# An mLSTM and MLP kernel: the output stores of steps 2 to 6 go from ScalarE's DMA queue to SyncE's

## The chip, the cores and the metric

The kernel runs on one core of a Trainium2 chip. The metric is device time in microseconds for one execution, lower being better. A core has a matrix engine (TensorE, PE), three engines for elementwise work (VectorE or DVE, ScalarE or ACT, GpSimd or POOL) and SyncE (SP), which here does nothing but issue DMAs. Each engine runs its own stream of instructions in order. A DMA is issued by an instruction in the stream of one of them (ACT's and SP's here); the transfer itself runs on 16 DMA engines, which both streams share.

## The reference

The input holds 4 batches of 8 heads with 768 time steps and head size 40. For each head an mLSTM recurrence runs over the time steps, with gates in the log domain and a running maximum for stability. Its output, 3072 rows (batch and time) of 320 values, goes through an MLP of width 2048:

```python
for t in range(S):
    m_new = np.maximum(f_gate[:, :, t] + m, i_gate[:, :, t])
    f_stab = np.exp(f_gate[:, :, t] + m - m_new)
    i_stab = np.exp(i_gate[:, :, t] - m_new)
    C = f_stab * C + i_stab * outer(v[t], k[t])      # per batch and head
    n = f_stab * n + i_stab * k[t]
    y[t] = sigmoid(o_gate[t]) * (C @ q[t]) / max(abs(n @ q[t]), 1)
...
h = x @ w_in          # x: y as (3072, 320), w_in (320, 2048)
g = h * sigmoid(h)
out = g @ w_out       # w_out (2048, 320)
```

All inputs and the output are float32.

## The kernel before

**Units and steps.** The recurrence is done in chunks of 64 time steps (`L`). There are 12 chunks and two pairs of batches, so 24 units; a unit holds one chunk of two batches and all heads, 128 rows of the MLP's input. Three units (`UPS`) make a step: 384 rows that go through the MLP together. There are 8 steps (`NSTEP`), numbered 0 to 7 by `j`.

**The MLP in a step.** The width 2048 is cut into 16 groups of 128, counted by `fc`. For each group `mm1` (L743) makes `ph`, 128 x 384, in a PSUM bank; `act` makes the gated value from it: the tanh on ACT (L750), `(th + 1) * ph` on DVE (L764), and from step 1 on a split into a rounded high part `gh` (ACT, L769) and the low rest `gl` (DVE, L773). `mm2` (L794) then multiplies with `w_out` and accumulates over all 16 groups into three PSUM banks `pout`, one for each 128 rows. It runs two groups behind `mm1` (`LAG`), so the last two groups of step `j` are multiplied while `fc` is 0 and 1 in step `j + 1`. In steps 1 to 7 three matmuls stand for one product, to keep float32 accuracy.

**The store.** When the last group of a step has been accumulated, which is at `fc = 1` of the next step, `store` copies each `pout` bank to SBUF as `ob` (ACT, L814; the very last copy of all is on DVE, L812) and issues two DMAs of 64 rows each (L818), one for each batch of the pair. So a step has three copies and six stores. `ob` has three buffers, except in the last step, which takes larger ones from another pool. The three `pout` banks are written again by `mm2` of the new step at `fc = 2`, and each must have been copied by then. Before the change, the stores of steps 0 and 1 are issued by SP, those of steps 2 to 6 by ACT, and in step 7 one of each two by SP and the other by ACT.

**The units in between.** The attention units of step `j + 1` are worked on inside step `j`: in steps 1 to 6 at `fc` 2, 7 and 12 (`PLACES`). There `block` puts the unit's matmuls on TensorE (scores L511, values L583 and L598, state L648), `close` and the calls after it do the weighting (L538), the norm (L611 to L621) and `x` (L635) on DVE, and `carry` updates the state (POOL L668, DVE L674). One group later `turn` transposes `x` on TensorE (L690), and ACT and DVE put it down as the high and low input of the next step (L701, L702). The first of these three places comes right behind the stores of the step before.

**What sets the order.** The order on each engine is the order in which the code is written; all engines are scheduled by hand. On SP, `turn(n)` issues the loads for unit `n + 3`: two DMAs for `D` (L430), one for `qk` (L438), one for `ko` (L445), two for `vb` (L451), and then two for `lq` of unit `n + 2` (L464). Buffers are few: `D`, `ko` and `vb` rotate over three, `lq` over two, so a load waits until a unit before it has been read. The weights are loaded and prepared in step 0 and partly step 1. After the last units (21 to 23) are reached, `turn` has fewer loads to issue, and step 7 has none.

What each engine does around a step boundary, in written order: TensorE has `mm1(0)`, `mm2(14)` of the old step, `mm1(1)`, `mm2(15)` of the old step, `mm1(2)`, the unit's matmuls, `mm2(0)`, `mm1(3)`, `mm2(1)`, the transposes. ACT has the three copies with whatever DMA issues stand behind each, then the tanh of `fc = 2`, `gh`, and so on.

Of the kernel before, what the change touches and what calls it, by code (L numbers as in the profile page):

```python
# [29 lines left out]
NSTEP = NU // UPS  # L30
# [13 lines left out]
def mlstm_mlp_kernel(  # L44
# [11 lines left out]
    nc = tc.nc  # L56
# [649 lines left out]
    class Step:  # L706
# [97 lines left out]
        def store(self, t):  # L804
            n = self.j * UPS + t
            c, p = n // NP, n % NP
            if self.j < NSTEP - 1:
                ob = p3.tile([128, DM], F32, tag="ob", name=f"ob{n}")
            else:
                ob = pb.tile([128, DM], F32, tag="big", name=f"ob{n}")  # L810
            if self.j == NSTEP - 1 and t == UPS - 1:
                nc.vector.tensor_scalar(ob, self.po[t], 0.5, None, op0=ALU.mult)  # L812
            else:
                nc.scalar.activation(ob, self.po[t], AF.Copy, scale=0.5)  # L814
            for k in range(2):
                r = (2 * p + k) * S + c * L
                q = nc.sync if self.j in (0, 1) or self.j == NSTEP - 1 and k == 0 else nc.scalar
                q.dma_start(out[r : r + L, :], ob[k * L : (k + 1) * L])  # L818


# [281 lines left out]
```

## Time and profile before

| | |
|---|---|
| median of 3 executions | 464.67 us (464.63 to 466.96) |
| the profiled execution | 465.99 us |
| its span, first to last instruction | 464.1 us |
| mean granted TensorE clock | 0.989 of full speed |
| busy share of PE, DVE, ACT, POOL | 96%, 58%, 46%, 25% |

How such rows are read. In a row of the timeline the first number is the start in microseconds from the span's start, the second the duration, then the engine, the line of the code, the operation and its tiles, a count where several were merged, and in brackets how long the engine had been idle before and what ended that. ACTq and SPq are the sequencers of ACT and SP, so a row with ACTq and DMA_DIRECT2D is a DMA being issued, not its transfer. In a row of the waits stand the waiting engine and line, what it waited for, the total in microseconds, how often, and the longest. In a row of windows stand the window, its length, then busy time and number of instructions for PE, PEld (weight loads), DVE, ACT and POOL, and at the end the granted TensorE clock, the mean busy share of the DMA engines and GB/s. A row of a line gives the shortest, median and longest duration in nanoseconds and the first and the last start. The chain of work is followed back from the last instruction to what released it.

### The profile page before, as it was taken

Reading aid. Unit: us, or ns where it says so; the run is one execution under the profiler, and the core shown is the slowest. Engines: PE = TensorE matmul, PEld = TensorE weight load, DVE = VectorE, ACT = ScalarE, POOL = GpSimd, SP = SyncE. Lnnn points to the kernel's source line nnn. Section 1 sums busy time; section 2 is a strip of 40 time slices with the busy share of each in tenths; the row PEclk is TensorE's granted clock in tenths of the full one; section 3 lists DMA queues with packets and bytes.
Section 4 is the critical chain, followed back from the end, with each engine's and each line's share of the span. In section 5 each row is a group of like instructions: output and inputs, shape, how many; then the busy total and the mean of one; then the engine's idle time right before and its main releaser. Section 6 shows DMA issues by size and latency. Waiting matters only on the chain.

```text
span 464.1 us, 11033 instructions
## 1 busy us (share of the span) xinstructions
PE 445.1 (96%) x4477; PEld 408.8 (88%) x4477; DVE 269.8 (58%) x609; ACT 212.1 (46%) x442; POOL 115.6 (25%) x123
## 2 busy tenths in 40 slices
PE   7899999999999999979999899998999899999995
PEld 3667677899999999979999799998999799998995
DVE  5777799578775566444664555636655355533342
ACT  6674856444753442525424344434344344333332
POOL 4224234134142234131431332322332311000000
PEclk9899999999999999998999999999999999998999
DMA  8999896361331442141430522413313200001001
GB/s 211 320 295 274 235 265 148 97 159 49 81 122 40 127 122 65 59 110 56 124 101 22 148 63 76 123 48 118 122 31 93 62 1 2 2 12 32 0 1 42
DMA packets 27314, 47.03 MB, mean 101 GB/s; under 512 B 4160, under 2 KB 14464, under 8 KB 27264
## 3 DMA queue, kind: packets, MB, share of 16 engines
q1 hardware_dynamic: 24224, 43.45, 33.6%
q10 hardware_dynamic: 3040, 2.89, 2.3%
q8 instruction: 35, 0.57, 0.5%
q14 instruction: 15, 0.12, 0.1%
HBM read 42.30 MB, written 4.01 MB: 100 GB/s over the span
## 4 chain that ended last, share of the span: by engine, by line
PE 83%; DMA 6%; DVE 3%; ACTq 3%; ACT 2%; issue 1%; SPq 0%; DVEq 0%
PE ph L743 37%; PE pout L794 35%; DMA wro<-in_w_out_dram 3%; ACTq L818 3%; PE p L598 3%; DMA qk<-in_qk_dram 3%; PE p L511 2%; PE pu L648 2%; PE p L583 2%; PE p L690 2%; ACT ob L814 1%; ACT th L750 1%; DVE th L764 1%; DVE D L538 1%; PE pt L193 0%
## 5 line engine op out<-in xcount | busy, mean ns | idle before, releaser
L750 ACT ACTIVATE th<-ph 128x384 f32<-128x384 f32 x128 | 62.4, 487 | 139.8 <-PE ph L743 132.7
L764 DVE SCALAR_TENSOR_TENSOR th<-th,ph 128x384 f32<-128x384 f32 x112 | 62.1, 555 | 107.5 <-ACT th L750 106.9
L743 PE MATMUL ph<-xh,wh 128*128 128x384 f32 x336 | 116.3, 346 | 0.0
L743 PE MATMUL ph<-xl,wh 128*128 128x384 f32 x336 | 114.6, 341 | 0.0
L794 PE MATMUL pout<-woh,gh 128*128 128x320 f32 x336 | 106.5, 317 | 2.2 <-ACT ob L814 2.2
L794 PE MATMUL pout<-woh,gl 128*128 128x320 f32 x336 | 104.2, 310 | 0.0
L794 PE MATMUL pout<-wol,gh 128*128 128x320 f32 x336 | 103.7, 308 | 0.0
L773 DVE TENSOR_TENSOR gl<-th,gh 128x384 fp32r<-128x384 f32 x112 | 64.6, 577 | 47.5 <-ACT gh L769 47.5
L769 ACT CAST gh<-th 128x384 fp32r<-128x384 f32 x112 | 57.5, 513 | 74.9 <-DVE th L764 74.3
L743 PE MATMUL ph<-xh,wl 128*128 128x384 f32 x224 | 76.6, 342 | 0.0
L794 PEld LDWEIGHTS pout<-woh,gh 128*128 128x128 f32 x336 | 63.6, 189 | 5.5 <-ACT ob L814 3.4
L495 POOL TENSOR_TENSOR qt<-qk,lq 104x512 f32<-104x512 f32 x22 | 29.5, 1340 | 141.5 <-ACT lq L491 125.0
L743 PEld LDWEIGHTS ph<-xl,wh 128*128 128x128 f32 x336 | 63.8, 190 | 0.2
L743 PEld LDWEIGHTS ph<-xh,wh 128*128 128x128 f32 x336 | 63.7, 190 | 0.2
L794 PEld LDWEIGHTS pout<-wol,gh 128*128 128x128 f32 x336 | 63.5, 189 | 0.0
L794 PEld LDWEIGHTS pout<-woh,gl 128*128 128x128 f32 x336 | 63.5, 189 | 0.0
L668 POOL TENSOR_TENSOR Cm<-Cm,lq 40x328 f32<-40x328 f32 x40 | 30.2, 756 | 114.5 <-PE p L598 113.0
L743 PEld LDWEIGHTS ph<-xh,wl 128*128 128x128 f32 x224 | 42.6, 190 | 0.0
L794 PE MATMUL pout<-wo,g 128*128 128x320 f32 x96 | 28.8, 436 | 0.6 <-DVE wo L261 0.6
L482 POOL TENSOR_TENSOR D<-D,am 128x512 f32<-128x512 f32 x20 | 25.8, 1288 | 7.4 <-DMA D<-LFd 5.4
L474 POOL TENSOR_TENSOR am<-mask,aT 128x512 f32<-128x512 f32 x20 | 23.2, 1160 | 7.8 <-DVE aT L203 6.3
L743 PE MATMUL ph<-x,wi 128*128 128x384 f32 x64 | 23.8, 494 | 0.0
(113 smaller groups left out, 485.6 us busy)
## 6 DMA issues: line engine op xcount, KB each, us to landing
qk<-in_qk_dram SPq DMA_DIRECT2D x24, 416.0 KB
ko<-in_ko_dram SPq DMA_DIRECT2D x24, 320.0 KB
wro<-in_w_out_dram SPq DMA_DIRECT2D x8, 640.0 KB
D<-LFd SPq DMA_DIRECT2D x40, 128.0 KB
wri<-in_w_in_dram SPq DMA_DIRECT2D x8, 512.0 KB
vb<-in_vp_dram SPq DMA_DIRECT2D x48, 82.0 KB
out_dram<-ob ACTq DMA_DIRECT2D x33, 80.0 KB
lq<-LFd SPq DMA_DIRECT2D x20, 128.0 KB
```

Of the source, the lines that this page charges most:

```text
L474: nc.gpsimd.tensor_tensor(out=self.am, in0=mask.unsqueeze(1).broadcast_to([128, H, L]), in1=aT[:, self.c, self.p, :].unsqueeze(2).broadcas ...
L482: nc.gpsimd.tensor_tensor(out=self.Dm, in0=self.Dm, in1=self.am, op=ALU.add)
L495: nc.gpsimd.tensor_tensor(out=self.qt, in0=self.q, in1=self.lq, op=ALU.mult)
L598: nc.tensor.matmul(self.out[g * L : (g + 1) * L, d, :, e, :], self.qt[:, j, :], cm[:, :, j, :], start=False, stop=True, skip_group_check=True,
L668: nc.gpsimd.tensor_tensor(out=v, in0=v, in1=self.lq[r, :, L - 1].unsqueeze(2).broadcast_to([D, H, D1]), op=ALU.mult,)
L743: nc.tensor.matmul(ph, w, x, start=(i == 0), stop=(i == len(ops) - 1))
L750: nc.scalar.activation(th, ph, AF.Tanh, scale=0.5)
L764: nc.vector.scalar_tensor_tensor(out=th, in0=th, scalar=1.0, in1=ph, op0=ALU.add, op1=ALU.mult)
L769: nc.scalar.copy(gh, th)
L773: nc.vector.tensor_tensor(out=gl, in0=th, in1=gh.bitcast(F32), op=ALU.subtract)
L794: nc.tensor.matmul(self.po[t], g[:, ts], w, start=(fc == 0 and i == 0), stop=(last and i == len(ops) - 1),)
L818: q.dma_start(out[r : r + L, :], ob[k * L : (k + 1) * L])
```

## The change

The condition that picks the issuing engine of a store is shortened. Every store of steps 0 to 6 is now issued by SP; in step 7 it stays as it was. The copies, the tiles, the sizes and all other instructions are the same, and the order in which the code writes them down is the same on all engines.

```diff
@@ -814,7 +814,7 @@
                 nc.scalar.activation(ob, self.po[t], AF.Copy, scale=0.5)
             for k in range(2):
                 r = (2 * p + k) * S + c * L
-                q = nc.sync if self.j in (0, 1) or self.j == NSTEP - 1 and k == 0 else nc.scalar
+                q = nc.sync if self.j < NSTEP - 1 or k == 0 else nc.scalar
                 q.dma_start(out[r : r + L, :], ob[k * L : (k + 1) * L])
```

## The prediction

> **What bounds the kernel now.** I read the page first: the busy shares and the chain of work that ended last.
>
> ```profile
> span 464.1 us, 11033 instructions
> PE 445.1 (96%) x4477; PEld 408.8 (88%) x4477; DVE 269.8 (58%) x609; ACT 212.1 (46%) x442; POOL 115.6 (25%) x123
> ...
> PE ph L743 37%; PE pout L794 35%; DMA wro<-in_w_out_dram 3%; ACTq L818 3%; PE p L598 3%; DMA qk<-in_qk_dram 3%; PE p L511 2%; PE pu L648 2%; PE p L583 2%; PE p L690 2%; ACT ob L814 1%; ACT th L750 1%; DVE th L764 1%; DVE D L538 1%; PE pt L193 0%
> ```
>
> TensorE sets the time; what can be won is the part of the span in which it idles or is clocked down. But L818, the line that issues the stores, stands on the chain with 3% as ACTq: ScalarE's sequencer issuing DMAs. So the next views are where those issues are made, and who makes TensorE wait between 190 and 430 us:
>
> ```profile
> L818 ACTq DMA_DIRECT2D out_dram<-ob x33: 472/549/1674, 197.4 to 460.6; - x33
> L818 SPq DMA_DIRECT2D out_dram<-ob x15: 502/587/1656, 92.7 to 460.6; - x15
> ```
> ```profile
> PE p L690 <- DVE x L635: 7.1, 4, 2.4
> PE pout L794 <- ACT ob L814: 2.2, 4, 1.0
> ```
>
> One issue holds its queue for a median 549 ns on ACT, 587 ns on SP. From 190 us on TensorE waits twice four times, 9.3 us together; the same question over 90 to 196 us has no row at all. Eight steps of 128x3 rows each end in six stores, and the stores of steps 0 and 1 are on SP already. So the trace holds the changed order too: the step boundaries at 92 and 145 us have their stores on SP, those at 197, 254, 308, 362 and 415 us on ACT. The timeline of one of each kind, SP's first:
>
> ```profile
> 144.76 1.08 ACT L814 ACTIVATE ob<-pout 128x320 f32<-128x320 f32 x3
> 145.22 4.82 SPq L818 DMA_DIRECT2D out_dram<-ob  x6
> 145.96 0.49 ACT L750 ACTIVATE th<-ph 128x384 f32<-128x384 f32 x1
> 150.12 1.19 SPq L430 DMA_DIRECT2D D<-LFd  x2
> 150.16 0.68 DVE L635 SCALAR_TENSOR_TENSOR x<-ko,p 128x256 f32<-128x256 f32 x3
> 152.30 0.49 PE L690 MATMUL p<-ident,x 128*128 128x128 f32 x3
> ```
> ```profile
> 196.99 0.43 ACT L814 ACTIVATE ob<-pout 128x320 f32<-128x320 f32 x1
> 197.45 1.19 ACTq L818 DMA_DIRECT2D out_dram<-ob  x2
> 198.76 0.44 ACT L814 ACTIVATE ob<-pout 128x320 f32<-128x320 f32 x1 [1.34 <-PE ph L743]
> 200.94 0.44 ACT L814 ACTIVATE ob<-pout 128x320 f32<-128x320 f32 x1 [1.74 <-PE pu L648]
> 203.35 0.49 ACT L750 ACTIVATE th<-ph 128x384 f32<-128x384 f32 x1 [1.97 <-DMA out_dram<-ob]
> 207.28 0.55 PE L690 MATMUL p<-ident,x 128*128 128x128 f32 x3 [2.44 <-DVE x L635]
> ```
>
> With the stores on SP, ACT copies all three output tiles in 1.08 us and starts the next tanh (L750) 1.20 us after the first copy. With the stores on ACT, two issues stand behind each copy and the tanh starts 6.36 us after it. The releasers printed there (ph, pu) had long been done; the time between the copies is the issues. VectorE runs in written order: its L764 needs that tanh, the norm of the attention unit stands behind it, x comes last, and TensorE's transposes (L690) wait 2.44 us.
>
> **The change part by part.** Thirty issues (steps 2 to 6, six each) go from ACT to SP. No instruction, tile or byte is added. The gain per boundary is read by windows from the first output copy to the transposes, all with the same 128 to 130 matmuls (the last has no unit, below):
>
> ```profile
> 92.21:100.04 7.83, 7.83 (x130) 7.42 (x130) 5.86 (x16) 3.09 (x8) 4.02 (x4) 1.00 0.41 102
> 144.76:152.30 7.54, 7.54 (x129) 7.12 (x128) 5.51 (x14) 2.57 (x7) 4.01 (x4) 1.00 0.34 88
> 196.99:207.28 10.29, 7.85 (x129) 7.00 (x128) 3.83 (x12) 2.70 (x7) 3.81 (x4) 1.00 0.41 118
> 253.59:263.40 9.81, 7.97 (x129) 7.02 (x127) 3.83 (x12) 2.70 (x7) 3.81 (x4) 1.00 0.42 122
> 308.15:317.08 8.93, 7.70 (x129) 7.02 (x127) 3.83 (x12) 2.70 (x7) 3.82 (x4) 1.00 0.46 134
> 361.86:371.93 10.07, 7.96 (x129) 7.03 (x128) 3.83 (x12) 2.69 (x7) 3.80 (x4) 1.00 0.27 72
> ```
>
> The first number is the window's length, the second TensorE's busy time in it. In the two SP boundaries these are equal: nothing is left to win there. I take 7.54 as the price of a changed boundary, because the one at 92 us holds two split instructions of the first weights besides; 7.83 is the upper bound. The four excesses are 2.75 + 2.27 + 1.39 + 2.53 = 8.94 us (7.78 by the upper bound).
>
> What follows each stall, from the transposes to the next first copy:
>
> ```profile
> 152.30:196.99 44.69, 44.69 (x444) 43.85 (x442) 24.94 (x55) 19.54 (x42) 11.94 (x11) 1.00 0.33 92
> 207.28:253.59 46.31, 46.31 (x442) 45.47 (x443) 26.28 (x57) 19.63 (x42) 11.94 (x11) 0.96 0.26 77
> 263.40:308.15 44.75, 44.75 (x442) 43.91 (x443) 26.19 (x57) 19.42 (x42) 11.94 (x11) 1.00 0.29 80
> 317.08:361.86 44.78, 44.77 (x442) 43.94 (x443) 25.80 (x56) 19.41 (x42) 11.94 (x11) 1.00 0.27 80
> ...
> 209.00:211.00 2.00, 2.00 (x8) 2.00 (x8) 1.22 (x3) 1.16 (x3) 0.00 (x0) 0.50 0.74 259
> ```
>
> After the 2.44 us stall the granted clock (last but two) falls to 0.50, and the stretch takes 46.31 instead of 44.69: 1.62 us. The others lose 0.06 and 0.09, which I leave out. Without a stall no row shows such a drop, so I count 1.62.
>
> The last boundary (step 6 to 7) has no unit in it; its matmuls are read singly:
>
> ```profile
> 413.36 0.31 PE L794 MATMUL pout<-woh,gh 128*128 128x320 f32 x1
> 414.68 0.34 PE L743 MATMUL ph<-xh,wh 128*128 128x384 f32 x1
> 416.09 0.31 PE L794 MATMUL pout<-woh,gh 128*128 128x320 f32 x1
> 419.06 0.42 PE L794 MATMUL pout<-woh,gh 128*128 128x320 f32 x1 [1.00 <-ACT ob L814]
> 419.63 0.52 PE L743 MATMUL ph<-xh,wh 128*128 128x384 f32 x1
> 423.87 0.34 PE L743 MATMUL ph<-xh,wh 128*128 128x384 f32 x1
> ```
>
> Nine pout matmuls take 414.68 - 413.36 = 1.32 us, eight ph ones 416.09 - 414.68 = 1.41. From 416.09 to 423.87 lie pout, ph, pout: 4.05 us of work in 7.78, so 3.73 lost, partly to waiting for the copies (a PSUM bank is written again only once it is copied), partly to the halved clock (0.52 us against 0.34 for one matmul). With three copies in 1.08 us from 415.15 on, all banks are free at 416.23, before the second is due; I count the whole 3.73. Its lower bound is the waits alone, 2.2.
>
> A rule of the Trainium skill bears on the clock: TensorE: Matmul & The Clock Gate (Part 1: The HAM clock gate) has the clock halve after an idle window of about 3.4 us, free-running. The trace agrees on the half (0.50) but drops after 2.44 us of idling. By that rule neither gap would need to cost anything, and the drop terms (1.62, and about 1.5 of the 3.73) would be luck of the phase; the sum would be near 11.2 us and the time 454.8, inside the range.
>
> **What the move costs on SP.** The six issues hold SP 4.82 us there (3.7 to 4.8 in the two boundaries), and behind them in SP's order stand the loads of the next turn: D, qk, ko, the two halves of vb, lq. They cannot pass a store that waits for its copy.
>
> ```profile
> SPq L430 <- PE p L583: 125.7, 13, 11.4
> SPq L445 <- DVE x L635: 33.9, 13, 6.2
> ```
> ```profile
> 167.20 1.29 POOL L482 TENSOR_TENSOR D<-D,am 128x512 f32<-128x512 f32 x1
> ```
>
> Both first loads wait in any case, D's for the unit's matmuls (L583) and ko's for x. In the SP boundary the D load is issued at 150.12 to 151.31, some 3 us later in the boundary than it could be, and its first reader is POOL at 167.20: 15.9 us of cover. lq, issued last, is wanted two mm1 groups after the next unit and has about as much (estimate from the spacing of 2.73 us). So I cost the move at nothing; the bounds are 0 and, if the cover were gone, the 4.82 us per boundary. After step 5 only the lq load of the last unit remains, after step 6 none.
>
> **Sum:** 8.94 + 1.62 + 3.73 = 14.29 us, between 7.78 + 2.2 = 10.0 and 14.3. The profiled execution took 465.99 (span 464.1 and 1.9 around it): 465.99 - 14.29 = 451.7. The median is 464.67, 1.3 below it: 450.4 if that is an offset of the profiled run, 451.7 if it is one clock drop more, which the change would remove too. I take the middle, **451.0**.
>
> **The rivals.**
>
> 1. *A remainder stays* (chance 0.08). x then comes late from VectorE's own chain. In the SP boundary x is done at 150.84 and TensorE wants it at 152.30: 1.46 us of slack. Were x later than that by 1 us in four boundaries, with one clock drop and the lower 2.2 in the last, 14.29 - 4 - 1.62 - 1.53 = 7.14 remain, 7.15 less than counted: 451.0 + 7.15 = 458.2. For it: ACT and DVE alternate tightly. Against: two boundaries without any wait.
>
> 2. *The transfer is hidden anyway* (0.03). ACT is busy 46%, so the issues could lie in its idle time and the waits have another cause: 464.7. Against it stand the 1.97 us which the tanh waits for the stores, and the undisturbed SP boundaries. This is what the Trainium skill would lead one to: DMA: Bandwidth & Descriptors (Issuing engines are not separate DMA queues) says that the choice of issuer saves only the sequencer's time, usually small beside the DMA. Six issues in an engine's in-order stream are what this trace shows to be not small.
>
> 3. *Slower* (0.03): SP becomes the bound. Loads behind the stores arrive after their reader, POOL's L482, then the exponential, the weighting and the block on TensorE slip. The point is a delay of 15.9 us; past it each microsecond is paid at the four boundaries that load, so 19.5 us late (4 x 3.6 = 14.4) ends even and, 5 us past the point, 451.7 + 20 = 472. SP's queue shows 4.82 us of stores, a third of the cover.
>
> 4. *The stores stay tied to ACT* (0.01), by a wait that the written order keeps: as before, 464.7.
>
> **How the numbers follow.** The forecast has 0.85. Its own range is 449 to 454 (the median's 450.4 less a little, up to 10.0 us of gain less 451.7's offset: 465.99 - 10.0 = 456.0 at the most). The full range 449 to 456.5 takes those bounds in and leaves about 0.15 out: the rivals. About 0.5%, 2.3 us, is what a measurement can tell from no change. Faster 0.93 (forecast and rival 1), same 0.04 (2 and 4), slower 0.03 (3).
>
> **What would show it.** On ACT, three copies back to back and the tanh 1.2 us after the first at all seven boundaries; no row of PE waiting for x or ob after 190 us; windows of 7.5 us at the four boundaries and a granted clock of 1.00 after them; 45 stores on SPq, three on ACTq. L818 leaves the chain but for the tail. Wrong would be a POOL or ACT wait on D, lq or qk after a boundary, an x still late, or a clock drop without a stall.

## The result, and the profile after

The changed kernel takes 451.72 us (median of 4, 451.30 to 453.48) against 464.93 for the kernel before (median of 4, 464.63 to 466.96). The ratio is 0.9714, 95% interval 0.9676 to 0.9752: some 2.9% faster. The forecast was 451.0 in a range of 449.0 to 456.5. The profiled execution took 451.44 us, and the sum in the prediction, made against the profiled execution before, gave 451.7 for it.

The page of the changed kernel, busy shares and the chain by line:

```profile
span 449.6 us, 11053 instructions
...
PE 439.1 (98%) x4477; PEld 405.3 (90%) x4477; DVE 270.9 (60%) x609; ACT 211.5 (47%) x442; POOL 116.2 (26%) x123
...
PE ph L743 40%; PE pout L794 39%; PE p L598 3%; DMA wro<-in_w_out_dram 3%; DMA qk<-in_qk_dram 3%; PE p L511 3%; PE pu L648 2%; PE p L583 2%; PE p L690 2%; PE pt L193 0%; ACT ob L814 0%; DVE wo L261 0%; ACT wro L260 0%; ACTq L818 0%; SPq L107 0%
```

L818 on ACTq has gone from 3% of the chain to none, and the waits of TensorE between 80 and 450 us have no row left. The stores now stand on SP's queue, but for three in step 7:

```profile
L818 SPq DMA_DIRECT2D out_dram<-ob x45: 466/587/1665, 92.7 to 446.2; - x45
L818 ACTq DMA_DIRECT2D out_dram<-ob x3: 497/550/792, 444.5 to 446.2; - x3
```

The boundary behind step 2, in the timeline:

```profile
197.00 1.08 ACT L814 ACTIVATE ob<-pout 128x320 f32<-128x320 f32 x3
198.19 0.49 ACT L750 ACTIVATE th<-ph 128x384 f32<-128x384 f32 x1
...
197.45 3.99 SPq L818 DMA_DIRECT2D out_dram<-ob  x6
201.54 2.07 SPq L430 DMA_DIRECT2D D<-LFd  x2
...
204.54 0.49 PE L690 MATMUL p<-ident,x 128*128 128x128 f32 x3
```

The three copies stand back to back, the tanh starts 1.19 us after the first (6.36 before), and the transposes come without a wait. The windows from the first copy to the transposes at the four changed boundaries with a unit (columns as before: window, length, busy time by engine, granted clock, DMA share, GB/s):

```profile
197.00:204.54 7.54, 7.54 (x130) 7.12 (x129) 5.52 (x14) 2.57 (x7) 4.01 (x4) 1.00 0.33 86
249.25:256.80 7.55, 7.55 (x130) 7.13 (x129) 5.52 (x14) 2.58 (x7) 4.02 (x4) 1.00 0.36 98
301.48:309.02 7.54, 7.54 (x129) 7.12 (x128) 5.51 (x14) 2.57 (x7) 4.02 (x4) 1.00 0.36 92
353.74:361.28 7.54, 7.54 (x129) 7.12 (x128) 5.51 (x14) 2.58 (x7) 4.02 (x4) 1.00 0.33 87
```

They equal the 7.54 us of the undisturbed boundary of before, so 10.29 + 9.81 + 8.93 + 10.07 us has become 30.17: 8.93 us. The stretch behind the first of them and the last step, from its first copy to that of the next:

```profile
204.54:249.25 44.71, 44.71 (x444) 43.87 (x442) 24.94 (x55) 19.53 (x41) 11.94 (x11) 1.00 0.34 92
404.42:444.07 39.65, 39.65 (x251) 39.65 (x250) 16.14 (x29) 15.16 (x32) 0.00 (x0) 1.00 0.05 13
```

The first was 46.31 before (1.60 less), the second 43.37:

```profile
415.15:458.52 43.37, 41.70 (x251) 41.18 (x250) 16.14 (x29) 15.38 (x32) 0.00 (x0) 0.96 0.05 12
```

That is 3.72 less. 8.93 + 1.60 + 3.72 = 14.25 of the 14.5 us between the two spans.

**What varies, and what doesn't.** The first output copy of all comes between 92.1 and 95.8 us in the executions of this study, though nothing differs between the kernels up to there. From that copy on the same code takes the same time within some 0.03 us: step 1, for example, is 52.22 or 52.23 us whenever its two boundaries are undisturbed. So the experiments below are read by windows that start at a copy, and the medians, which also hold the spread of the beginning, stand beside them. Each experiment ran in a round with the kernel before, whose median was between 463.86 and 466.39 us in these rounds, so medians of different rounds are comparable to some tenths of a per cent only.

### The profile page after: what moved, and what is told of

Read it like the earlier page. It is cut to its first block, busy times and chain, and to the rows that moved or that the text cites. A ratio compares the mean times of both kernels' runs of the same rounds, so it can differ in the third digit from the quotient of the medians.

```text
span 449.6 us, 11053 instructions
## 1 busy us (share of the span) xinstructions
PE 439.1 (98%) x4477; PEld 405.3 (90%) x4477; DVE 270.9 (60%) x609; ACT 211.5 (47%) x442; POOL 116.2 (26%) x123
## 4 chain that ended last, share of the span: by engine, by line
PE 92%; DMA 6%; ACT 0%; issue 0%; DVE 0%; ACTq 0%; SPq 0%
PE ph L743 40%; PE pout L794 39%; PE p L598 3%; DMA wro<-in_w_out_dram 3%; DMA qk<-in_qk_dram 3%; PE p L511 3%; PE pu L648 2%; PE p L583 2%; PE p L690 2%; PE pt L193 0%; ACT ob L814 0%; DVE wo L261 0%; ACT wro L260 0%; ACTq L818 0%; SPq L107 0%
## 5 line engine op out<-in xcount | busy, mean ns | idle before, releaser
L794 PE MATMUL pout<-woh,gh 128*128 128x320 f32 x336 | 105.4, 314 | 0.0
L773 DVE TENSOR_TENSOR gl<-th,gh 128x384 fp32r<-128x384 f32 x112 | 65.6, 586 | 47.5 <-ACT gh L769 47.5
L794 PEld LDWEIGHTS pout<-wo,g 128*128 128x128 f32 x96 | 17.7, 189 | 7.3 <-DVE wo L261 1.9
```

The source lines that it names most:

```text
L773: nc.vector.tensor_tensor(out=gl, in0=th, in1=gh.bitcast(F32), op=ALU.subtract)
L794: nc.tensor.matmul(self.po[t], g[:, ts], w, start=(fc == 0 and i == 0), stop=(last and i == len(ops) - 1),)
```

## The experiments

**One boundary put back, behind step 2.**

```diff
-                q = nc.sync if self.j < NSTEP - 1 or k == 0 else nc.scalar
+                q = nc.sync if self.j != 2 and (self.j < NSTEP - 1 or k == 0) else nc.scalar
```

> The changed kernel, but the six stores of step 2 go out on ACT again, so one boundary (near 197 us) is as it was before. Theory (the issues in ACT's in-order stream delay the tanh, and with it x): that boundary takes 10.3 us again instead of 7.5, and where the clock drops after it 1.6 more; 451.7 + 2.75 = 454.5, or 456.1 with the drop. Rival (what was won does not sit at the single boundary, but comes from ACT's queue being busy over the whole span): a fifth of the gain, 13.2 / 5 = 2.6 us, without any wait of TensorE for x.

Measured: 455.66 us. The window of that boundary and the stretch behind it:

```profile
199.67:209.20 9.53, 7.85 (x129) 7.00 (x128) 3.82 (x12) 2.71 (x7) 3.81 (x4) 1.00 0.45 127
209.20:253.98 44.78, 44.78 (x442) 43.94 (x443) 26.19 (x57) 19.41 (x42) 11.95 (x11) 1.00 0.28 80
```

TensorE waits 1.7 us for x once, there and nowhere else; the other boundaries keep their 7.54. The loss sits at the boundary. But it is 1.99 us, not 2.75, and the clock does not drop after it. The median alone would not show this: it is 3.9 us above that of the changed kernel, and in the profiled execution 2.7 us of the difference lie ahead of the first copy (94.90 us against 92.22).

**The boundary without a unit put back, behind step 6.**

```diff
-                q = nc.sync if self.j < NSTEP - 1 or k == 0 else nc.scalar
+                q = nc.sync if self.j < NSTEP - 2 or self.j == NSTEP - 1 and k == 0 else nc.scalar
```

> The changed kernel, but the six stores of step 6 go out on ACT again (the boundary without an attention unit). Theory: TensorE waits twice for the output copies, 0.7 and 1.0 us and twice less, in all 2.2 us, and 1.5 more if the clock drops: 453.9 to 455.4. Rival (no unit, so no chain over DVE, and TensorE makes the waits good later): 451.7.

Measured: 454.73 us, and the last step by the same window as above:

```profile
404.48:446.37 41.89, 40.16 (x251) 39.64 (x250) 16.05 (x29) 15.27 (x32) 0.00 (x0) 1.00 0.05 13
```

41.89 - 39.65 = 2.24 us, at full clock. So of the 3.72 us gained there, 2.2 are the waits for the copies, and about 1.5 were the clock drop of that one execution. TensorE waits twice here, not four times:

```profile
406.74 0.41 PE L794 MATMUL pout<-woh,gh 128*128 128x320 f32 x1 [0.73 <-ACT ob L814]
408.45 0.42 PE L794 MATMUL pout<-woh,gh 128*128 128x320 f32 x1 [1.01 <-ACT ob L814]
```

The two gaps are 1.74 us. The other 0.5 us are in how the rows count: the matmuls are shown as 0.31 us long but start about 0.15 us apart, so a wait costs more than the gap that is shown.

**Half of the stores on ACT.**

```diff
-                q = nc.sync if self.j < NSTEP - 1 or k == 0 else nc.scalar
+                q = nc.sync if self.j < 2 or k == 0 else nc.scalar
```

> In steps 2 to 6 each tile's first store goes out on SP and its second on ACT: three issues on ACT for each boundary instead of six or none. Theory (a chain with slack): each copy is followed by one issue of 0.55 us, the tanh comes some 1.7 us later than in the changed kernel, against 1.46 us of slack ahead of the transposes; 0.2 to 0.8 us lost in each of five boundaries, 452.5 to 455.5. Rival (the loss is in proportion to the issues on ACT): half of 13.2 us, 458.3.

Measured: 453.54 us. The timeline of ACT and the window at the boundary behind step 2:

```profile
198.01 0.43 ACT L814 ACTIVATE ob<-pout 128x320 f32<-128x320 f32 x1
201.17 0.49 ACT L750 ACTIVATE th<-ph 128x384 f32<-128x384 f32 x1 [0.58 <-PE p L598]
```
```profile
198.01:205.55 7.54, 7.54 (x129) 7.12 (x128) 4.28 (x12) 2.80 (x7) 4.01 (x4) 1.00 0.45 110
```

The tanh is 3.16 - 1.20 = 1.96 us later (1.90 to 1.96 at the four boundaries with a unit), and the window is 7.54 all the same at all four. Only the last step loses 0.97 us (40.62). So three issues are free where a unit's work lies between, six are not: no proportion, a slack, and one larger than the 1.46 us that I had counted.

**All seven boundaries on ACT.** Here the kernel before is changed instead:

```diff
-                q = nc.sync if self.j in (0, 1) or self.j == NSTEP - 1 and k == 0 else nc.scalar
+                q = nc.sync if self.j == NSTEP - 1 and k == 0 else nc.scalar
```

> The kernel before, but the stores of steps 0 and 1 go out on ACT as well, so that all seven boundaries have them there. Theory: the two boundaries near 92 and 145 us, undisturbed so far, lose what the others lost, 1.4 to 2.8 us each and up to 1.6 for the clock: 465 + 3 to 9 = 468 to 474. Rival (these two are undisturbed for another reason, since the weights are still being prepared there): 465, and their windows stay at 7.5 to 7.8 us.

Measured: 467.3 us (median of 10), against the kernel before 1.0026, 0.9998 to 1.0054: no difference that is clear of noise. The two boundaries that had been undisturbed:

```profile
93.60:102.55 8.95, 7.99 (x130) 7.31 (x130) 4.17 (x13) 3.31 (x8) 3.82 (x4) 1.00 0.48 135
147.33:157.30 9.97, 7.97 (x130) 7.04 (x128) 3.83 (x12) 2.70 (x7) 3.80 (x4) 1.00 0.46 121
```

They went from 7.83 and 7.54 to 8.95 and 9.97, as the theory has it. The total missed its range: some 1.2 us more than the kernel before, where at least 3 were expected. The four later windows of this execution came out 1.36 us shorter together than those of the kernel before (37.74 us against 39.10), and there was one clock drop fewer. All six windows of boundaries with a unit are longer than undisturbed ones, by 1.1 to 2.5 us, but of the seven boundaries only one is followed by a clock drop, the one behind step 5:

```profile
374.11:418.87 44.76, 44.76 (x378) 43.95 (x379) 22.08 (x49) 18.04 (x38) 2.61 (x2) 0.96 0.01 1
```

In the kernel before the same boundary had the same window of 10.07, and the stretch behind it took 43.22 at full clock; there drops came behind step 2 and step 6 instead.

With these, the windows can be set against the tanh. Late means later than in the undisturbed boundary, from the first copy on:

| kernel, boundary behind step | tanh late | window longer | late less longer |
|---|---|---|---|
| before, 2 / 3 / 4 / 5 | 5.16 / 4.68 / 3.80 / 4.94 | 2.75 / 2.27 / 1.39 / 2.53 | 2.41 each |
| step 2 alone on ACT, 2 | 4.40 | 1.99 | 2.41 |
| all on ACT, 0 / 1 | 3.54 / 4.84 | 1.12 / 2.43 | 2.42 / 2.41 |
| all on ACT, 2 / 3 / 4 / 5 | 3.80 / 4.66 / 3.82 / 4.94 | 1.39 / 2.25 / 1.41 / 2.53 | 2.41 each |
| half on ACT, 2 | 1.96 | 0 | (not reached) |

In these eleven boundaries there are 2.41 us of slack, and each microsecond of the tanh beyond it is paid in full.

**On ACT's queue, but later in the order.** Each store of steps 2 to 6 is put on a list, and the next step issues one of them at each of six groups:

```diff
+                if 2 <= self.j < NSTEP - 1:
+                    later.append((out[r : r + L, :], ob[k * L : (k + 1) * L]))
+                    continue
...
             else:
                 st.act(fc, splits=[SPLITS[x[0]](int(x[1])) for x in LOWS.get((j, fc), ())])
+            if fc in (5, 6, 10, 11, 14, 15) and later:
+                nc.scalar.dma_start(*later.pop(0))
```

> The thirty stores stay on ACT's queue, but are issued later in the written order: one each behind the rounding copy (L769) at groups 5, 6, 10, 11, 14 and 15 of the next step. Theory (the place in ACT's stream costs, not the queue): ACT has 1.1 us of idle time there and an issue takes 0.55, so nothing waits: 451.7, within 1 us of the changed kernel. Rival (ACT's issuing costs wherever it stands): 465 or near it.

Measured: 453.04 us, 0.9757 of the kernel before (0.9718 to 0.9796). TensorE waits for nothing after 95 us, and the windows are those of the changed kernel. One issue in the timeline of ACT:

```profile
214.29 0.51 ACT L769 CAST gh<-th 128x384 fp32r<-128x384 f32 x1 [0.62 <-DVE th L764]
214.29 0.47 ACTq L1017 DMA_DIRECT2D out_dram<-ob  x1
215.91 0.49 ACT L750 ACTIVATE th<-ph 128x384 f32<-128x384 f32 x1 [1.10 <-PE ph L743]
```

The next tanh still waits only for its matmuls. So the queue as such costs nothing; thirty issues at ACT's idle places are as good as thirty on SP.

**The stores on GpSimd.**

```diff
+                if 2 <= self.j < NSTEP - 1:
+                    q = nc.gpsimd
```

> The thirty stores of steps 2 to 6 go out on GpSimd's queue. Theory (a store costs where what stands behind it in its stream is wanted soon): POOL's work at a boundary, the scaling of the state (L668) and the add for D (L482), stands behind the stores, with about 2 us of its own slack; six issues of 0.5 to 1.5 us from the first copy on would push it back by 0 to 6 us: 451.7 to 470. No row so far shows what an issue takes there. Rival (only ACT's stream is tight): 451.7, whatever an issue takes.

Measured: 452.61 us (median of 2). The stores' line and the first changed window:

```profile
L820 POOL DMA_DIRECT2D out_dram<-ob x30: 521/523/707, 197.7 to 407.7; - x30
```
```profile
196.94:204.49 7.55, 7.55 (x130) 7.13 (x129) 5.52 (x14) 2.59 (x7) 6.56 (x10) 1.00 0.56 154
```

An issue takes 0.52 us there, POOL's work at the boundary comes about 1 us later, and its own slack takes that. This run does not tell the theory from its rival; it shows a third place for the stores.

**SP's cover: more and more issues.** Each store of steps 2 to 6 is cut into m pieces by rows, with m = 2, 4, 8 and 16:

```diff
-                q.dma_start(out[r : r + L, :], ob[k * L : (k + 1) * L])
+                m = 8 if 2 <= self.j < NSTEP - 1 else 1
+                for s in range(0, L, L // m):
+                    q.dma_start(out[r + s : r + s + L // m, :], ob[k * L + s : k * L + s + L // m])
```

> The changed kernel with each store of steps 2 to 6 cut into two of 32 rows: twelve issues on SP for each boundary. Theory (SP's issues are covered by 15.9 us until the D load's first reader): some 3.5 us more on SP, no change, 451.7. Rival (SP is near its limit): each further microsecond on SP is paid at four boundaries, up to 451.7 + 14 = 466.

> The same with four pieces of 16 rows: 24 issues for each boundary, 14 us at 0.59 us each, so the loads behind them come 9 to 10 us later than in the changed kernel. Theory: still inside the cover of 15.9 us, 451.7 to 452.5. Rival: 451.7 + 4 x 9 = 488 at the most.

> The same with eight pieces of 8 rows: 48 issues, 28 us at 0.59 us each, the loads 22 to 23 us later. Theory: past the cover of 15.9 us by some 6 to 7 us at the boundaries behind steps 2, 3 and 4 (behind step 5 only one load is left), with waits of POOL for the D load: 451.7 + 3 x 6 = 470, less if an issue of few rows takes less than 0.59 us. Rival (the loads' readers have far more cover than that): 451.7.

> Each store of steps 2 to 6 cut into sixteen pieces of 4 rows: 96 issues on SP for each boundary, some 28 us if they take the 0.30 us that pieces of 8 rows took. With 48 issues POOL waited 0.48 us for the D load, whose issue began 18.6 us after the first copy; so the load may begin 18.1 us after it and no later. Theory (SP's stores cost nothing up to that point and then each microsecond counts): the load begins 28 us after the copy, 10 late; POOL's wait is 10 us, of which 3.4 are covered by the gap between POOL's add and ACT's exponential; 6 to 10 us are lost behind each of steps 2, 3 and 4: 470 to 482. Rival (the readers give way, or the loads pass the stores): 451.7 to 454.

| pieces | issues at a boundary | us on SP (step 2) | D load begins, after the copy | step 2 | median |
|---|---|---|---|---|---|
| 1 | 6 | 3.99 | 4.54 | 52.25 | 451.72 |
| 2 | 12 | 7.08 | 7.63 | 52.26 | 454.22 |
| 4 | 24 | 12.75 | 13.30 | 52.26 | 452.28 |
| 8 | 48 | 18.05 | 18.61 | 52.26 | 453.72 |
| 16 | 96 | 33.50 | 34.06 | 69.30 | 517.53 |

Up to 48 issues nothing is paid: in the profiled executions steps 1 to 6 are the same within 0.02 us and the difference lies in the beginning. My numbers for 48 missed: pieces of 8 rows take 0.30 us at the median and 0.38 on average, not 0.59, so SP was through after 18.05 us instead of 28. But that run stands just at the edge, as POOL's add for D shows, first with 48 issues, then with 96, and after it the window of step 2 with 96:

```profile
222.26 1.28 POOL L482 TENSOR_TENSOR D<-D,am 128x512 f32<-128x512 f32 x1 [0.48 <-DMA D<-LFd]
```
```profile
235.41 1.26 POOL L482 TENSOR_TENSOR D<-D,am 128x512 f32<-128x512 f32 x1 [15.40 <-DMA D<-LFd]
```
```profile
197.65:266.95 69.30, 56.77 (x571) 54.93 (x570) 30.36 (x68) 22.30 (x48) 15.90 (x15) 0.88 0.26 69
```

The load may begin 18.61 - 0.48 = 18.1 us after the copy; it begins at 4.5 in the changed kernel. That is 13.6 us of cover until POOL waits. With 96 issues it begins 16 us too late and step 2 takes 17.05 us more: TensorE is idle for 69.30 - 56.77 = 12.5 us, and its busy time is 4.5 longer at a granted clock of 0.88. I had expected 6 to 10, with the load 10 late: an issue took 0.35 us and the clock was not in the sum. Of the 29.5 us by which the load begins later than in the changed kernel, 12.5 show as idle time of TensorE, so some 17 us are covered before time is lost. The total, 517.53, missed the expected 470 to 482 by far more than step 2 explains. Steps 3 and 4 lost 16.20 and 15.88 us. Step 5, which I had left out, lost 10.09, with ACT waiting 8.9 us for the one load left there (`lq`). The tail behind the last first copy grew from 5.5 to 11.5 us, as SP is busy with the stores of steps 6 and 7 until 512.9 us. The mechanism is that of the third rival.

**Between three and six.** To test the slack, four issues on ACT:

```diff
-                q = nc.sync if self.j < NSTEP - 1 or k == 0 else nc.scalar
+                q = nc.sync if self.j < 2 or self.j < NSTEP - 1 and t == 2 or self.j == NSTEP - 1 and k == 0 else nc.scalar
```

> In steps 2 to 6 the first two tiles' stores go out on ACT and the third's on SP: four issues on ACT for each boundary. The eleven disturbed boundaries seen so far keep one rule: the window from the first copy to the transposes grows by what the tanh comes late beyond 2.41 us. Theory (that rule): the tanh comes 2.5 to 3.1 us later than the 1.20 of the changed kernel, so four windows of 7.6 to 8.2 us instead of 7.54, and at the last boundary the third bank is copied as late as before, 1.7 to 2.2 us: 453.5 to 456. Rival (each issue on ACT costs the same): four sixths of the six issues' loss, windows of 8.5 to 9.5 us, 457 to 460.

Measured: 461.24 us (median of 5; the profiled execution 458.43). The tanh is 2.83, 2.49, 2.48 and 3.30 us late, and the window is 8.64 each time. The rule would have given 7.96, 7.62, 7.61 and 8.43, so it failed as it stood. The median lies above both forecasts, and the profiled execution inside the rival's. 8.64 lies in the rival's range too, but a cost for each issue does not explain why four different delays end in one number. The timeline of VectorE and of POOL at the first two boundaries:

```profile
203.18 1.19 DVE L773 TENSOR_TENSOR gl<-th,gh 128x384 fp32r<-128x384 f32 x1
256.29 1.53 DVE L773 TENSOR_TENSOR gl<-th,gh 128x384 fp32r<-128x384 f32 x1
...
202.66 1.30 POOL L482 TENSOR_TENSOR D<-D,am 128x512 f32<-128x512 f32 x1
256.10 1.30 POOL L482 TENSOR_TENSOR D<-D,am 128x512 f32<-128x512 f32 x1
```

gl, which stands ahead of x, takes 1.19 and 1.53 us here, and both times it ends 0.41 us after POOL's add does (204.37 after 203.96, 257.82 after 257.40). The add itself ends 7.05 us after the first copy (203.96 - 196.91), and within 0.01 us of that at the other three boundaries, whenever the tanh comes. The last run takes that add away, nearly, beside the edit above:

```diff
-            nc.gpsimd.tensor_tensor(out=self.Dm, in0=self.Dm, in1=self.am, op=ALU.add)
+            nc.gpsimd.tensor_tensor(
+                out=self.Dm[:, 0:1], in0=self.Dm[:, 0:1], in1=self.am[:, 0:1], op=ALU.add
+            )
```

> The same four issues on ACT, and POOL's add for D (L482) is done for one head of eight instead of all (the other seven heads' mask and gate term are left out of the result), so that it takes some 0.2 us instead of 1.30. With four issues the window came out as 8.64 at all four boundaries, whether the tanh came 2.5 or 3.3 us late, and VectorE's gl (L773) took 1.19 and 1.53 us instead of 0.51, ending 0.41 us after POOL's add each time. Theory (gl and POOL's add cannot run at once, and the add's end sets x): gl takes 0.5 us again and the windows follow the tanh: 7.54 plus what it comes late beyond 2.41, so 7.6 to 8.4. Rival (gl is long for another reason, the store issues or the transfers): gl stays at 1.2 to 1.5 us and the windows at 8.64.

Measured: 457.62 us (median of 2). The timeline of gl (L775 here, as the edit adds two lines) and POOL's add, and the first three windows:

```profile
204.16 0.51 DVE L775 TENSOR_TENSOR gl<-th,gh 128x384 fp32r<-128x384 f32 x1
...
203.63 0.33 POOL L482 TENSOR_TENSOR D<-D,am 128x64 f32<-128x64 f32 x1
```
```profile
197.89:205.84 7.95, 7.70 (x129) 7.03 (x127) 3.82 (x12) 2.69 (x7) 2.85 (x4) 1.00 0.33 86
250.62:259.37 8.75, 7.97 (x129) 7.03 (x128) 3.83 (x12) 2.70 (x7) 2.85 (x4) 1.00 0.32 83
304.12:311.77 7.65, 7.65 (x129) 7.02 (x127) 3.87 (x12) 2.69 (x7) 2.84 (x4) 1.00 0.29 68
```

gl is back at 0.51 to 0.56, and the windows follow the tanh again: late by 2.83, 3.62 and 2.48 us, longer by 0.41, 1.21 and 0.11 (the fourth is as the third). So the slack of 2.41 us holds unless VectorE comes to gl while POOL has its add; then the add's end sets x.

## Why the prediction was right, point by point

- **What bounds.** Shown: with the issues off ACT's stream TensorE waits for nothing, with them back at one boundary it waits there, and with the two good boundaries made like the others these fall too. That it is the place in the stream and not ACT's queue is shown by the late issues.
- **The four windows, 8.94 us.** Measured 8.93. The price of 7.54 was right, the bound of 7.83 was that of step 0's other work. Only this price was at stake: the lengths before are rows of the execution that the sum was made from. In other executions the stores on ACT cost other amounts; the boundary behind step 2 took 10.29 us in the kernel before, 9.53 with step 2 alone on ACT and 8.93 with all on ACT.
- **The clock, 1.62 us and a part of 3.73.** Right in size for this pair of executions (1.60, and 3.72 for the last boundary, of which 2.2 are waits). That the lower bound, 2.2, came out is luck: it was the total of the row over 190 to 430 us, four waits, of which two (1.7 us) lie at the last boundary and two (0.6 us) inside the four windows, where they were counted already; the 2.24 us were read as a difference of windows. And the step "without a stall no row shows such a drop, so I count 1.62" took for the price of a stall what is the luck of an execution: of the 14 boundaries with six issues on ACT (five before, seven with all on ACT, one in each of the two kernels with one put back) three were followed by a drop, and boundaries with equal windows differ. The rule of the Trainium skill that stood beside the row (TensorE: Matmul & The Clock Gate, Part 1) has the clock halve after an idle window of about 3.4 us, free-running. These gaps are at most 2.44 us, and 11 of the 14 boundaries agree with it in having no drop; the three with one do not follow from it, and what decides there stays open. In this pair of executions 8.93 + 2.24 = 11.2 us of the 14.25 are waits and the rest is drops.
- **SP's cost, nothing.** Right, with 13.6 us to spare until a reader waits. The step said 15.9: it counted from the end of the load's issue to its reader and left out the time of the landing.
- **The time.** 451.44 and 451.72 against 451.7 by the profiled execution's own sum. The middle of two sums, 451.0, was the worse choice: the median of 464.67 is not the profiled execution less a constant. That the sum met the profiled execution to 0.3 us has luck in it: both profiled executions have their first copy at 92.2 us, others up to 95.8, and the sum had no term for that.
- **First rival.** Did not happen. Its 1.46 us of slack were x's alone and too small; 2.41 was measured. In the undisturbed boundary VectorE also waits 0.66 us for the unit's matmuls ahead of L538, and gl takes 0.76 instead of 0.51 beside POOL; 1.46 + 0.66 + 0.25 = 2.37, all of which a late tanh would use up first (an estimate from these rows; no run separates the three). **Second and fourth:** fell. **Third:** its mechanism exists, at 48 to 96 issues instead of 6; its point, a delay of 15.9 us, lies between the 13.6 at which POOL first waits and the some 17 at which time is lost.

## What to carry to other kernels

A DMA issue of half a microsecond is part of the in-order stream it stands in: look at what stands behind it and how soon that is wanted, not at the busy share of its engine. Where a kernel holds the same boundary in two arrangements, their windows give the gain directly. Before moving issues, measure the slack on both sides, here 2.41 us on ACT and 13.6 us on SP; a cost in proportion to the number of issues is the wrong picture, since up to the slack they are free and beyond it they are paid. And the slack holds for one order of events: with four issues on ACT another wait, that for POOL's add, came into its place.

## What the runs showed of the hardware

- **The time of an issue varies, and the cause stays open.** With all stores on ACT, a pair of issues takes 1.12 us at one copy, and 2.18 at the next, where SP issues the D load at the same moment. In the kernel before, a pair behind step 5 takes 2.19 us while SP issues nothing (third row):

```profile
147.79 1.12 ACTq L818 DMA_DIRECT2D out_dram<-ob  x2
149.51 2.18 ACTq L818 DMA_DIRECT2D out_dram<-ob  x2
```
```profile
364.03 2.19 ACTq L818 DMA_DIRECT2D out_dram<-ob  x2
```
```profile
149.57 2.12 SPq L430 DMA_DIRECT2D D<-LFd  x2
```

Such long pairs are why the tanh was 3.8 us late at one boundary and 5 at another. That two sequencers slow each other is not shown: the D load takes 2.07 us in the changed kernel behind step 2, where ACT issues nothing, and 1.10 in the kernel before at 199.22 us, beside a pair on ACT. The Trainium skill has one generator of descriptors, locked for exclusive use (Perfetto Trace Analysis, DMA Instruction — HWDGE (DVE, Sync)); no run here tested whether such a lock is what lengthens an issue.

- **A VectorE operation can wait for one on GpSimd without any wait being shown:** gl took 1.19 and 1.53 us beside POOL's add and 0.51 without. The Trainium skill names a port pair that a VectorE instruction with two SBUF inputs and a GpSimd one that reads SBUF share, the later one blocking fully (SBUF — State Buffer, SBUF: two separate sides); gl has two such inputs, and the trace agrees, as gl ends 0.41 us after the add.

- **The clock in the first 30 us differs from execution to execution** of the same code, here 20 to 28 us in the changed kernel and in the one with twelve issues. The rows are windows as above; the last but two is the clock:

```profile
20.00:24.00 4.00, 3.85 (x52) 2.72 (x52) 2.95 (x11) 3.23 (x11) 1.45 (x2) 1.00 1.04 286
24.00:28.00 4.00, 4.00 (x45) 2.69 (x44) 2.56 (x8) 1.70 (x4) 1.56 (x2) 1.00 1.03 306
```
```profile
20.00:24.00 4.00, 2.99 (x46) 2.27 (x44) 3.61 (x14) 1.72 (x5) 0.00 (x0) 0.61 0.95 273
24.00:28.00 4.00, 4.00 (x29) 2.83 (x27) 1.69 (x7) 2.79 (x9) 1.84 (x3) 0.54 0.99 297
```

The first copy comes at 92.22 us in the one and at 95.81 in the other: 3.6 us, as much as the two profiled executions differ (451.44 and 454.89). That the clock alone makes this difference is not shown: in the kernel before it was 0.57 from 20 to 24 us, and the first copy still came at 92.22. What sets a drop off in one execution and not in another stays open.
